# Decode attention with a gated feed-forward: the query projection with x stationary, and two row blocks of the output weight loaded behind the last V piece

## The chip, the cores and the metric

The kernel runs on one core of a Trainium2 chip. Its metric is the device time of one execution in microseconds (us). Most executions of one kernel lie within 0.4 us of its median here, under 0.02%. Differences under 2% count as "the same". A profile's span runs from the first to the last instruction and is about 1.8 us shorter than the device time.

PE is the matrix engine (PEld are its weight loads), DVE the vector engine, ACT the scalar engine, and SP the engine that issues the loads. PSUM is the memory that matmuls write. Each load leaves 16 landing records in the trace, called its shares here; it has landed with the last of them. The granted clock is the part of PE's full clock that the profile shows as granted. The single landing records and DMA packets quoted below are read from the trace itself; no view prints them one by one.

## The reference

One token x (512 values) goes through attention over a cache of 65,536 keys in 32 heads, and through a small gated feed-forward block. A gate g mixes both.

```python
x = A_x                                            # 1 x 1 x 512, bf16
g = sigmoid((x * gate_w).sum(-1))
q = (x @ wq).reshape(32, 128)                      # wq: 512 x 4096
p = softmax(q . k_cache * 128 ** -0.5)             # k_cache, v_cache: 32 x 65536 x 128
a = (p . v_cache).reshape(4096) @ wo               # wo: 4096 x 512
b = (silu(x @ w_gate) * (x @ w_up)) @ w_down       # 512 x 1792, 1792 x 512
out = g * a + (1 - g) * b
```

K and V together are 1,074 MB, the rest is 14 MB. Every byte is used once.

## The kernel before

There are three slots of 64 KB per partition. Each holds one chunk of K or V (32,768 keys, 8 MiB) at a time; every head has two chunks. SP issues all loads but two rows of 1 KB (x and gate_w, issued by ACT) in order, on one queue, and waits for a slot to come free before the next load.

```python
for n in range(N - 1):                 # N = 64 chunks
    load("k", n, [KPP]); load("v", n, [KPP])
    for j in range(0, KPP, m):
        block(n, j, m)                 # DVE: K *= q (in place); PE: identity as weight, 128 products per key summed to 8
        gather()                       # DVE: the sum of these 8; ACT: exp into P_sb
    pv(n)                              # PE: P stationary, 4 keys x 128 columns of V per matmul
```

Before that loop stands the q stage. Slot 0 holds wq, gate and up first; the load of chunk K1 into slot 0 waits until PE has read them. One column of PSUM takes one head; 128 blocks of wq are loaded as weights, with one column of x each:

```python
group("q_ps", [(m_x[:, h : h + 1],
                [(wq_sb[:, t, h * Dh : (h + 1) * Dh], Xc[:, t : t + 1]) for t in range(KT)])
               for h in range(H)], ...)
act("qT", qT, m_x[:, :H], ACT.Copy, ...)
def spread(h):                         # q of one head onto all partitions
    act("dq", dq, ident, ACT.Copy, scale=qT[:, h : h + 1])
    mms("spread", m_sp[:, :Dh], [(ones_b, dq)], ...)
    act("q_bc", q_bc[h % 2], m_sp[:, :Dh], ACT.Copy, ...)
# ... (cut)
gate()     # DVE, PE, ACT: g and 1 - g
hidden()   # PE: 112 matmuls on gate and up
```

At the end, the last V chunk comes in pieces, so that little work stands behind the last landing. The last two V chunks are multiplied by columns: V[:, j, :] is the weight, one column of P is streamed. The heads 0 to 30 go through wo early; only the last head's row block (`wo_last`) waits for the last V:

```python
V_END = [KPP // 2, KPP // 4, KPP // 8, KPP // 16, KPP // 16]      # 128, 64, 32, 16, 16 keys per partition
dma("wd", ...); dma("wo", wo, ...); dma("wl", wo_last[:, 0, :], ...)
load("k", n, [EK] * 4); load("v", n, V_END)
# ... (cut: row_b = (1-g) b; row_a = g * (31 heads) @ wo; rest4 = their sum, turned to 4 x 128)
column(n, V_END[:1]); sum_ps(h, H); norm(h, H)
column(n, V_END[1:], V_END[0])
dve("Z", ...)                                                      # last head's output / its sum
mms("l_ps", m_x[:OT, :P], [(Z[:, OT*q : OT*(q+1)], wo_last[:, 0, P*q : P*(q+1)]) for q in range(OT)], ...)
dve("out_sb", ...)                                                 # g * l_ps + rest4
dma("out", ...)
```

A helper (`Plan`) tracks reads and writes and adds the semaphore waits. It tracks a slot in units of 8 x 128 elements per partition, 2 KB.

The softmax here doesn't subtract the row's maximum and nothing guards it: scores larger than these inputs give would overflow.

## Time and profile before

| | before |
|---|---|
| time | 2518.3 us (2518.23 to 2518.3, 3 runs) |
| span of the profile | 2516.4 us |
| PE / DVE / ACT busy | 79% / 50% / 4% |
| data queue, mean over the span | 432 GB/s, 1088 MB |
| last landing of a load | 2511.84 us |
| start of the last DVE operation | 2513.59 us |

Lines of the page: busy share of the 16 DMA engines in 40 slices (tenths), GB/s in the same slices, and two of the queues (packets, MB, share).

```profile
DMA  9999999999999999999999999999999999999998
GB/s 423 433 433 432 434 435 433 438 433 434 433 433 433 434 435 435 435 433 433 433 433 435 434 433 432 435 436 434 435 433 433 433 433 435 434 436 433 434 433 376
...
q1 hardware_dynamic: 20456, 1087.78, 99.8%
q8 instruction: 12, 0.20, 0.0%
```

Every slice but the last is full. The last one moves 376 instead of about 433 GB/s. The instruction queue carries 12 packets of 16 KB.

The table of windows for stretches of the same run (us; busy time of PE, PEld, DVE, ACT, POOL; granted PE clock; DMA share; GB/s):

```profile
1000.00:2000.00 1000.00, 794.56 (x3430) 157.04 (x1818) 511.97 (x103) 37.76 (x154) 0.00 (x0) 0.91 1.00 434
2508.00:2510.00 2.00, 2.00 (x67) 2.00 (x67) 0.33 (x2) 0.00 (x0) 0.00 (x0) 0.50 0.75 307
2510.00:2512.00 2.00, 1.55 (x59) 1.47 (x56) 0.00 (x0) 0.00 (x0) 0.00 (x0) 0.50 0.17 66
2512.00:2514.00 2.00, 1.22 (x20) 0.76 (x19) 0.57 (x2) 0.00 (x0) 0.00 (x0) 0.50 0.00 0
```

The stream runs at 434 GB/s and thins out over the last 3 us. The landing records show how: the 16 shares of the last transfer land between 2508.82 and 2511.84 us. Had all finished together, that would have been near 2510.1 (the mean of the 16). So by this estimate better balance could give 1.7 us at most. The granted clock in the last 10 us is half.

The timeline of the start (start, duration, engine, what, idle before):

```profile
13.24 3.58 PE L285 MATMUL m_x<-Xc,slot_65 128*128 128x1 bf16 x128 [10.65 <-DMA slot_65<-in_A_wq_dram]
...
23.00 6.85 PE L285 MATMUL m_x<-Xc,slot_65 128*128 128x1 bf16 x112 [5.26 <-DMA slot_65<-in_B_w_up_dram]
29.88 0.33 SPq L181 DMA_DIRECT2D slot_65<-in_A_k_cache_dram  x1
...
32.76 8.69 DVE L344 TENSOR_TENSOR slot_66<-slot_66,q_bc_78 128x16384 bf16<-128x16384 bf16 x1 [1.53 <-DMA slot_66<-in_A_k_cache_dram]
```

PE works on q from 13.24, waits for the up weights until 23.00, and frees slot 0 for K1 at 29.88. The first product starts when the first half of K0 has landed.

The end, from the chain of waits (the chain that ended last, in order of time: start, duration, what):

```profile
2467.34 1.90 issue
...
2470.97 40.88 DMA slot_65<-in_A_v_cache_dram
...
2511.89 0.51 PE m_c L257 x13
...
2512.40 0.25 PE m_c L257 x3
...
2512.68 0.24 DVE Z L601
...
2512.96 0.60 PE m_x L257 x4
...
2513.59 0.34 DVE out_sb L613
```

The 40.9 us of DMA are the time in the queue of the last V piece. Behind its landing stand 16 columns, Z, four matmuls and the last DVE operation. And PE's own lines from the timeline there:

```profile
2507.84 0.18 PE L257 MATMUL m_c<-P_sb_84,slot_65 128*128 128x1 bf16 x1 [2.44 <-issue]
...
2511.89 0.75 PE L257 MATMUL m_c<-P_sb_84,slot_65 128*128 128x1 bf16 x16 [0.45 <-DMA slot_65<-in_A_v_cache_dram]
2512.96 0.59 PE L257 MATMUL m_x<-slot_66,Z 128*4 128x128 bf16 x4 [0.32 <-DVE Z L601]
```

The first line shows 2.44 us for which PE waited for nothing that the profile names. An instruction packet of 16 KB starts at 2505.4 in the DMA records, so PE had probably run out of program. The same happens at 2467.34 in the chain (1.90 us).

### The profile page before, as it was taken

The page shows a single profiled execution, that of the slowest core. Times are in us where ns is not written, and L with a number is a line of the kernel's source. Part 1 is how long each engine was busy: PE and PEld are TensorE (multiplying, and loading weights), DVE is VectorE, ACT ScalarE, POOL GpSimd, SP SyncE. Part 2 cuts the span into 40 slices and gives each one's busy share as a digit, 9 for nine tenths or more (in the row PEclk, how much of TensorE's full clock was granted, in tenths as well). Part 3 has the DMA queues.
Part 4 walks back from the last instruction along what each step waited for, and adds up shares of the span by engine and source line. Part 5 has one row for each costly group of instructions (what it writes and reads, how often), then busy time and mean ns, then how long its engine had stood idle before and what let it go on. Part 6 is the DMA issues. An engine that isn't in the chain of part 4 may idle for free.

```text
span 2516.4 us, 15594 instructions
## 1 busy us (share of the span) xinstructions
PE 1977.2 (79%) x9185; PEld 410.9 (16%) x5221; DVE 1268.3 (50%) x287; ACT 99.1 (4%) x402; POOL 1.9 (0%) x9
## 2 busy tenths in 40 slices
PE   4687877877778778778787787787877877877788
PEld 2111111111111111111111111111111111111113
DVE  3455355464553554645545546445455364464554
ACT  0000000000000000000000000000000000000000
POOL 0000000000000000000000000000000000000000
PEclk9888989989989989898898898998989989989898
DMA  9999999999999999999999999999999999999998
GB/s 423 433 433 432 434 435 433 438 433 434 433 433 433 434 435 435 435 433 433 433 433 435 434 433 432 435 436 434 435 433 433 433 433 435 434 436 433 434 433 376
DMA packets 20478, 1088.02 MB, mean 432 GB/s; under 512 B 2282, under 2 KB 2412, under 8 KB 2668
## 3 DMA queue, kind: packets, MB, share of 16 engines
q1 hardware_dynamic: 20456, 1087.78, 99.8%
q8 instruction: 12, 0.20, 0.0%
q14 instruction: 6, 0.05, 0.0%
q10 hardware_dynamic: 4, 0.00, 0.0%
HBM read 1087.77 MB, written 0.00 MB: 432 GB/s over the span
## 4 chain that ended last, share of the span: by engine, by line
DMA 47%; PE 39%; DVE 13%; ACT 0%; issue 0%; another core or an unknown queue 0%; SPq 0%
PE O_ps L257 17%; DMA slot_67<-in_A_k_cache_dram 16%; DMA slot_66<-in_A_k_cache_dram 15%; DMA slot_65<-in_A_k_cache_dram 14%; PE S_ps_103 L275 11%; PE S_ps_104 L275 9%; DVE slot_67 L344 4%; DVE slot_66 L344 4%; DVE slot_65 L344 3%; DMA slot_65<-in_A_v_cache_dram 2%; PE m_c L257 2%; DVE S_sb_82 L369 2%; PE S_ps_103 L285 1%; ACT P_sb_83 L294 0%; PE S_ps_104 L285 0%
## 5 line engine op out<-in xcount | busy, mean ns | idle before, releaser
L344 DVE TENSOR_TENSOR slot_67<-slot_67,q_bc_79 128x16384 bf16<-128x16384 bf16 (+1 forms) x28 | 208.2, 7469 | 145.4 <-DMA slot_67<-in_A_k_cache_dram 145.4
L369 DVE TENSOR_REDUCE S_sb_82<-S_ps_104 128x128 f32<-128x1024 f32 (+1 forms) x66 | 78.7, 1192 | 395.0 <-PE S_ps_104 L275 395.0
L344 DVE TENSOR_TENSOR slot_65<-slot_65,q_bc_78 128x16384 bf16<-128x16384 bf16 x22 | 190.2, 8688 | 140.5 <-DMA slot_65<-in_A_k_cache_dram 140.5
L344 DVE TENSOR_TENSOR slot_66<-slot_66,q_bc_78 128x16384 bf16<-128x16384 bf16 x22 | 190.3, 8689 | 120.1 <-DMA slot_66<-in_A_k_cache_dram 120.1
L344 DVE TENSOR_TENSOR slot_65<-slot_65,q_bc_79 128x16384 bf16<-128x16384 bf16 x20 | 172.9, 8688 | 120.0 <-DMA slot_65<-in_A_k_cache_dram 120.0
L344 DVE TENSOR_TENSOR slot_66<-slot_66,q_bc_79 128x16384 bf16<-128x16384 bf16 x20 | 172.9, 8688 | 119.2 <-DMA slot_66<-in_A_k_cache_dram 119.2
L344 DVE TENSOR_TENSOR slot_67<-slot_67,q_bc_78 128x16384 bf16<-128x16384 bf16 x20 | 172.9, 8688 | 119.2 <-DMA slot_67<-in_A_k_cache_dram 119.2
L275 PE MATMUL S_ps_103<-slot_67,ident 128*128 128x512 bf16 x680 | 193.8, 455 | 0.0
L275 PE MATMUL S_ps_103<-slot_65,ident 128*128 128x512 bf16 x651 | 186.1, 456 | 0.0
L275 PE MATMUL S_ps_103<-slot_66,ident 128*128 128x512 bf16 x651 | 183.5, 452 | 0.0
L257 PE MATMUL O_ps<-slot_67,P_sb_83 128*4 128x512 bf16 x704 | 153.7, 379 | 21.0 <-ACT P_sb_83 L294 18.3
L257 PE MATMUL O_ps<-slot_66,P_sb_84 128*4 128x512 bf16 x704 | 153.7, 379 | 19.3 <-ACT P_sb_84 L294 19.3
L257 PE MATMUL O_ps<-slot_65,P_sb_84 128*4 128x512 bf16 x640 | 139.7, 379 | 18.3 <-ACT P_sb_84 L294 18.3
L257 PE MATMUL O_ps<-slot_67,P_sb_84 128*4 128x512 bf16 x640 | 139.7, 379 | 18.3 <-ACT P_sb_84 L294 18.3
L257 PE MATMUL O_ps<-slot_65,P_sb_83 128*4 128x512 bf16 x640 | 139.7, 379 | 18.3 <-ACT P_sb_83 L294 18.3
L257 PE MATMUL O_ps<-slot_66,P_sb_83 128*4 128x512 bf16 x640 | 139.8, 379 | 17.5 <-ACT P_sb_83 L294 17.5
L275 PE MATMUL S_ps_104<-slot_67,ident 128*128 128x512 bf16 x680 | 150.7, 379 | 0.0
L275 PE MATMUL S_ps_104<-slot_66,ident 128*128 128x512 bf16 x651 | 143.9, 379 | 0.0
L275 PE MATMUL S_ps_104<-slot_65,ident 128*128 128x512 bf16 x651 | 143.9, 379 | 0.0
L285 PE MATMUL S_ps_103<-slot_65,ident 128*128 128x512 bf16 x21 | 12.8, 608 | 138.0 <-DVE slot_65 L344 138.0
L285 PE MATMUL S_ps_103<-slot_66,ident 128*128 128x512 bf16 x21 | 12.8, 608 | 131.0 <-DVE slot_66 L344 131.0
L285 PE MATMUL S_ps_103<-slot_67,ident 128*128 128x512 bf16 x24 | 13.9, 579 | 125.6 <-DVE slot_67 L344 125.6
(100 smaller groups left out, 720.4 us busy)
## 6 DMA issues: line engine op xcount, KB each, us to landing
slot_66<-in_A_k_cache_dram SPq DMA_DIRECT2D x2, 4096.0 KB, 34.9
slot_67<-in_A_k_cache_dram SPq DMA_DIRECT2D x4, 2048.0 KB, 30.3
slot_65<-in_A_wq_dram SPq DMA_DIRECT2D x1, 4096.0 KB, 12.2
slot_66<-in_A_wo_dram SPq DMA_DIRECT2D x1, 4096.0 KB, 32.4
slot_65<-in_A_v_cache_dram SPq DMA_DIRECT2D x1, 4096.0 KB, 37.1
slot_65<-in_A_v_cache_dram SPq DMA_DIRECT2D x1, 2048.0 KB, 40.3
slot_65<-in_B_w_gate_dram SPq DMA_DIRECT2D x1, 1792.0 KB, 16.0
slot_65<-in_B_w_up_dram SPq DMA_DIRECT2D x1, 1792.0 KB, 21.0
```

What stands on the lines that cost most here:

```text
L257: ins = nc.tensor.matmul(out_ap, lhsT=a, rhs=b, start=start and i == 0, stop=stop and i == len(pairs) - 1,)
L275: ins = nc.tensor.add_instruction(mybir.InstMatmult(name=nc.get_next_instruction_name(), engine=mybir.EngineType.PE, ins=[nc.tensor.lower_ ...
L285: ins = nc.tensor.matmul(out_ap, lhsT=a, rhs=b, start=first, stop=last)
L344: "products", lambda: nc.vector.tensor_tensor(out=w, in0=w, in1=q_rep, op=ALU.mult),
L369: lambda: nc.vector.tensor_reduce(out=S_sb[b][:, :m], in_=S_ps[r][:, :m, :], axis=AXIS.X, op=ALU.add),
```

## The change

Its intent: fewer PE instructions for q, x as the weight and wq streamed; less work and fewer bytes bound to the last V landing, by smaller last pieces and by putting 256 KB of wo behind them, where they may land while PE and DVE finish the last head. To find the space for q4, three one-row tiles share one, and both projections now end in one row. The diff is shortened: `...` and plain words stand for code that is cut.

```diff
-    group("q_ps", ... 32 heads x 4 matmuls, weights wq block, one column of x ...)
-    act("qT", qT, m_x[:, :H], ACT.Copy, ["m_x"], ["qT"])
+    group("q_ps",
+        [[(q_ps[32 * g : 32 * g + 1, i * W : (i + 1) * W],
+           [(x_col, wq_sb[:, t, (2 * g + i) * W : (2 * g + i + 1) * W]) for t, x_col in enumerate(x_cols)])
+          for i in range(2)] ... for g in range(OT)], units(0, 0, WQ) + ["Xc"], [("S_ps", 0)])
+    for g in range(OT):
+        act("q4", q4[32 * g : 32 * g + 1, :], q_ps[32 * g : 32 * g + 1, :], ACT.Copy, ...)
     def spread(h):
-        act("dq", dq, ident, ACT.Copy, ["ident", "qT"], ["dq"], scale=qT[:, h : h + 1])
-        mms("spread", m_sp[:, :Dh], [(ones_b, dq)], ["ones_b", "dq"], ["m_sp"])
+        g, i = divmod(h, QP)
+        act("dq", dq, q4[32 * g : 32 * g + 1, i * Dh : (i + 1) * Dh], ACT.Copy, [("q4", g)], ["dq"])
+        mms("spread", m_sp[:, :Dh], [(ones_b[0:1, :], dq)], ["ones_b", "dq"], ["m_sp"])
...
-    V_END = [KPP // 2, KPP // 4, KPP // 8, KPP // 16, KPP // 16]
+    V_END = [KPP // 2, KPP // 4, KPP // 8, KPP // 16, KPP // 32, KPP // 32]
...
-    dma("wo", wo, ..., units(ws, WO, WL))
+    dma("wo", wo[:, :ON, :], wo_rows[:, :ON, :], units(ws, WO, WO + ON * D))      # ON = H - LATE = 30
     dma("wl", wo_last[:, 0, :], ...)
     load("k", n, [EK] * (KPP // EK))
     load("v", n, V_END)
+    dma("wo2", wo[:, ON:, :], wo_rows[:, ON:, :], units(ws, WO + ON * D, WL))
...
-    row_b and row_a apart, 8 small matmuls for rest4
+    one row: ACT writes (1-g) b, DVE adds g a; 4 small matmuls for rest4
...
     column(n, V_END[1:], V_END[0])
+    mms("late_ps", m_x[:OT, :P], 8 matmuls of ZM with the two late row blocks, stop=False)
     dve("Z", ...)
     mms("l_ps", ..., start=False)
```

More of the change, by code (lines that the diff above doesn't have):

```diff
@@ L18 @@
 VB = 4
+LATE = 2
 R = 8
@@ L122 @@
     slot = [ring_pool.tile([P, SLOT], bf16, name=f"slot{i}") for i in range(SLOTS)]
-    x_row = sb("x_row", [1, D], bf16)
-    gw_row = sb("gw_row", [1, D], bf16)
+    row = sb("row", [1, 3 * D // 2], f32)
+    x_row, gw_row, xg = (row.bitcast(bf16)[:, i * D : (i + 1) * D] for i in range(3))
     ones = sb("ones", [P, P], f32)
@@ L130 @@
     Xc = sb("Xc", [P, KT], bf16)
-    qT = sb("qT", [P, H], f32)
-    dq = sb("dq", [P, Dh], bf16)
+    QP = H // OT
+    q4 = sb("q4", [P, QP * Dh], bf16)
+    dq = sb("dq", [1, Dh], bf16)
     q_bc = [sb(f"q_bc{i}", [P, Dh], bf16) for i in range(2)]
@@ L144 @@
     eg = sb("eg", [P, FT], f32)
-    xg = sb("xg", [1, D], bf16)
     s_t = sb("s_t", [1, 1], f32)
@@ L148 @@
     rest4 = sb("rest4", [OT, P], f32)
-    row_b = sb("row_b", [1, D], f32)
     unit = sb("unit", [1, OT * OT], f32)
     Z = sb("Z", [P, OT * OT], bf16)
+    ZM = sb("ZM", [P, LATE, OT * OT], bf16)
     o_row = sb("o_row", [H, Dh], bf16)
@@ L231 @@
     op("DVE", "unit1", lambda: nc.vector.memset(unit[:, :: OT + 1], 1.0), writes=["unit"])
+    op("DVE", "ZM0", lambda: nc.vector.memset(ZM, 0.0), writes=["ZM"])
     op("DVE", "Z0", lambda: nc.vector.memset(Z, 0.0), writes=["Z"])
@@ L269, in fn @@
             held = None
-            for out_ap, pairs in parts:
-                for i, (a, b) in enumerate(pairs):
-                    first, last = i == 0, i == len(pairs) - 1
-                    if a is held:
-                        ins = nc.tensor.add_instruction(
-                            mybir.InstMatmult(
-                                name=nc.get_next_instruction_name(), engine=mybir.EngineType.PE,
-                                ins=[nc.tensor.lower_ap(b), weights],
-                                outs=[nc.tensor.lower_ap(out_ap)],
-                                start_tensor_calc=first, stop_tensor_calc=last,
-                                tile_size=(P, P), tile_position=(0, 0), ldweights=False,
-                            )
-                        )
-                    else:
-                        ins = nc.tensor.matmul(out_ap, lhsT=a, rhs=b, start=first, stop=last)
-                        weights = ins.ins.ins[1]
-                    held = a
+            for part in parts:
+                part = part if isinstance(part, list) else [part]
+                for i in range(len(part[0][1])):
+                    for out_ap, pairs in part:
+                        a, b = pairs[i]
+                        first, last = i == 0, i == len(pairs) - 1
+                        if a is held:
+                            ins = nc.tensor.add_instruction(
+                                mybir.InstMatmult(
+                                    name=nc.get_next_instruction_name(),
+                                    engine=mybir.EngineType.PE,
+                                    ins=[nc.tensor.lower_ap(b), load.ins[1]],
+                                    outs=[nc.tensor.lower_ap(out_ap)],
+                                    start_tensor_calc=first, stop_tensor_calc=last,
+                                    tile_size=load.tile_size, tile_position=load.tile_position,
+                                    ldweights=False,
+                                )
+                            )
+                        else:
+                            ins = nc.tensor.matmul(out_ap, lhsT=a, rhs=b, start=first, stop=last)
+                            load = ins.ins
+                        held = a
             return ins
@@ L310 @@
     dve("Xc", lambda: nc.vector.tensor_copy(out=Xc, in_=m_x[:, :KT]), ["m_x"], ["Xc"])
+    q_ps = S_ps[0].rearrange("p k r -> p (k r)")
+    W = 512
+    assert QP * Dh == 2 * W
     group(
@@ L315 @@
         [
-            (
-                m_x[:, h : h + 1],
-                [(wq_sb[:, t, h * Dh : (h + 1) * Dh], Xc[:, t : t + 1]) for t in range(KT)],
-            )
-            for h in range(H)
+            [
+                (
+                    q_ps[32 * g : 32 * g + 1, i * W : (i + 1) * W],
+                    [
+                        (x_col, wq_sb[:, t, (2 * g + i) * W : (2 * g + i + 1) * W])
+                        for t, x_col in enumerate(x_cols)
+                    ],
+                )
+                for i in range(2)
+            ]
+            for x_cols in [[Xc[:, t : t + 1] for t in range(KT)]]
+            for g in range(OT)
         ],
-        units(0, 0, WQ) + ["Xc"], ["m_x"],
+        units(0, 0, WQ) + ["Xc"], [("S_ps", 0)],
     )
-    act("qT", qT, m_x[:, :H], ACT.Copy, ["m_x"], ["qT"])
+    for g in range(OT):
+        act("q4", q4[32 * g : 32 * g + 1, :], q_ps[32 * g : 32 * g + 1, :], ACT.Copy,
+            [("S_ps", 0)], [("q4", g)])
     def spread(h):
-        act("dq", dq, ident, ACT.Copy, ["ident", "qT"], ["dq"], scale=qT[:, h : h + 1])
-        mms("spread", m_sp[:, :Dh], [(ones_b, dq)], ["ones_b", "dq"], ["m_sp"])
+        g, i = divmod(h, QP)
+        act("dq", dq, q4[32 * g : 32 * g + 1, i * Dh : (i + 1) * Dh], ACT.Copy,
+            [("q4", g)], ["dq"])
+        mms("spread", m_sp[:, :Dh], [(ones_b[0:1, :], dq)], ["ones_b", "dq"], ["m_sp"])
         q = h % 2
@@ L474, in gate, with project @@
         )
-    def row(key, w_v, names, cols, cname, ks, bank, bname):
+    EARLY = ["x_row", "gw_row", "xg"]
+    def project(key, w_v, names, cols, cname, ks, bank, bname):
         mms(key, bank[0:1, :D], [(cols[:, k : k + 1], w_v[:, k, :]) for k in ks],
@@ L565 @@
     dma("wd", wd, B_w_down.rearrange("(p t) n -> p t n", t=FT), units(ws, 0, WO))
-    dma("wo", wo, A_wo.rearrange("(p t) n -> p t n", t=H), units(ws, WO, WL))
+    wo_rows = A_wo.rearrange("(p t) n -> p t n", t=H)
+    ON = H - LATE
+    dma("wo", wo[:, :ON, :], wo_rows[:, :ON, :], units(ws, WO, WO + ON * D))
     dma("wl", wo_last[:, 0, :], A_wo[(H - 1) * Dh :, :], units(ws, WL, WL + D))
@@ L569 @@
     load("v", n, V_END)
+    dma("wo2", wo[:, ON:, :], wo_rows[:, ON:, :], units(ws, WO + ON * D, WL))
     turn_outputs(0)
     turn_outputs(1)
-    row("b_ps", wd, units(ws, 0, WO), hT, "hT", range(FT), m_x, "m_x")
-    act("row_b", row_b, m_x[0:1, :D], ACT.Copy, ["m_x", "ngval"], ["row_b"], scale=ngval[0:1, :])
-    row("a_ps", wo, units(ws, WO, WL), M, "M", range(H), m_sp, "m_sp")
-    row_a = O_sb[0:1, :D]
-    act("row_a", row_a, m_sp[0:1, :D], ACT.Copy, ["m_sp", "gval"], ["O_sb"], scale=gval[0:1, :])
+    project("b_ps", wd, units(ws, 0, WO), hT, "hT", range(FT), m_x, "m_x")
+    act("row", row[:, :D], m_x[0:1, :D], ACT.Copy, ["m_x", "ngval"], ["row"] + EARLY,
+        scale=ngval[0:1, :])
+    project("a_ps", wo, units(ws, WO, WO + ON * D), M, "M", range(ON), m_sp, "m_sp")
     for i, j in enumerate(range(0, KPP, EK)):
-        if i == 2:
+        if i == 3:
             mms(
@@ L582 @@
                 [
-                    (unit[:, OT * q : OT * (q + 1)], r[:, P * q : P * (q + 1)])
-                    for r in (row_b, row_a)
+                    (unit[:, OT * q : OT * (q + 1)], row[:, P * q : P * (q + 1)])
                     for q in range(OT)
                 ],
-                ["unit", "O_sb", "row_b"], ["m_sp"],
+                ["unit", "row"], ["m_sp"],
             )
@@ L590 @@
         block(n, j, EK)
+        if i == 1:
+            dve(
+                "row2",
+                lambda: nc.vector.scalar_tensor_tensor(
+                    out=row[:, :D], in0=m_sp[0:1, :D], scalar=gval[0:1, :], in1=row[:, :D],
+                    op0=ALU.mult, op1=ALU.add,
+                ),
+                ["m_sp", "gval", "row"], ["row"],
+            )
         while len(todo) > 1:
@@ L593 @@
     gather()
+    for t in range(LATE):
+        dve(
+            "ZM",
+            lambda t=t: nc.vector.tensor_copy(
+                out=ZM[:, t, :: OT + 1], in_=M[:, ON + t : ON + t + 1].to_broadcast([P, OT])
+            ),
+            ["M"], ["ZM"],
+        )
     column(n, V_END[:1])
@@ L597 @@
     column(n, V_END[1:], V_END[0])
+    mms(
+        "late_ps", m_x[:OT, :P],
+        [
+            (ZM[:, t, OT * q : OT * (q + 1)], wo[:, ON + t, P * q : P * (q + 1)])
+            for t in range(LATE)
+            for q in range(OT)
+        ],
+        ["ZM"] + units(ws, WO + ON * D, WL), ["m_x"], stop=False,
+    )
     dve(
@@ L608 @@
         [(Z[:, OT * q : OT * (q + 1)], wo_last[:, 0, P * q : P * (q + 1)]) for q in range(OT)],
-        ["Z"] + units(ws, WL, WL + D), ["m_x"],
+        ["Z"] + units(ws, WL, WL + D), ["m_x"], start=False,
     )
```

## The prediction

> **What bounds the kernel.** The DMA stream. The page's slices show all 16 DMA engines at 9 tenths or more, except in the last slice; its queue part gives 1088 MB at a mean of 432 GB/s over 2516.4 us, and the table of windows shows 433 to 435 GB/s in every stretch from 100 to 2440 us. The Trainium skill ("DMA: Bandwidth & Descriptors", section "Where 436 GB/s comes from") puts the port ceiling of one core at 435 GB/s; the trace agrees. PE is busy 79%, DVE 50%, both with idle time that nobody waits for. The change moves no byte out of the stream, so only the ends can change: before the stream starts (about 2 us, untouched) and after its last landing. In the timeline the last V piece lands at 2511.84 and the span ends at 2516.44, 4.6 us later.
>
> **The start (q).** 128 weight loads with one-column matmuls took 3.58 us (from 13.24). Now 16 loads of x and 32 matmuls of 512 columns. In the trace such matmuls take 0.43 us on a PE coming from idle and 0.22 us later, so I estimate 8 to 10 us, then four one-partition copies on ACT (a 1x512 copy took 0.68 us, so about 1.1 us each). gexp, then the gate/up matmuls, queue behind these copies: they start near 27 instead of 23 us, the second K load is issued near 34 instead of 29.9, the first product starts near 36 instead of 32.8. The queue then still holds over 20 us of transfers (K0 and V0 end near 59). So this stage gets 3 to 4 us slower and costs nothing. The dq copies and spread in the loop are hidden.
>
> **The tail.** Before, after the landing: 16 columns and their wait 0.8 us, Z 0.27, four matmuls to their end 0.6: 1.70 us to the start of the last DVE operation. After: 256 KB of wo land last, at about the same time as the last V piece did, because the bytes are the same. V's last 8 keys land some 0.6 us (256 KB at 434 GB/s) earlier; their columns (8 x 26 ns) and Z fit before or beside the late matmuls. Behind the last landing stand 8 + 4 matmuls of 128 columns, at the 0.106 us start to start that the four had at the 0.50 granted clock there: 1.48 us. Gain about 0.2 us, at most 0.7 with a warm clock; one more DMA and smaller rows cost up to 0.2 us.
>
> **Side effect.** PE's program gets 210 instructions shorter (3088 to 2878). The Trainium skill ("Runtime: NRT & Kernel Launch", section "Instruction fetch mechanics") says blocks of 256 instructions; the trace agrees: PE stands still at the 2304th (2467.3 to 2469.2 us) and the 2816th instruction (2505.4 to 2507.8), with a 16 KB instruction packet each time. Each such packet holds one DMA engine up by about 1.1 us, which spreads the landings of one piece. The stall at 2505 moves to about column 113 of the last 128, where PE waits for V anyway. If that fetch comes late, up to 1.5 us are lost; if its engine is one that already lags, 1 us.
>
> **Time.** 2517.9 us, 2516.3 to 2519.4 eight times in ten. Faster by over 2%: 0.005; within 2%: 0.99; slower: 0.005.
>
> **Right if:** the DMA rate stays 434 GB/s; the first product starts 2 to 5 us later yet K1 and V1 land when they did; the chain of waits ends in the landing of the wo piece, then matmuls, then the output DMA. **Wrong if:** a fetch stall falls behind the last landing, the DMA queue runs dry near 59 or 78 us, or the two-kilobyte rows slow the last slice.

## The result

The changed kernel took 2518.27 us (median of 6 runs, 2517.99 to 2518.45), the kernel before 2518.28 (6 runs, 2518.08 to 2519.59). The ratio is 0.9999 with a 95% interval of 0.9986 to 1.0012: the same. Ratios here are the mean time of one kernel's fast runs over that of the other's of the same rounds, so not quite the ratio of the medians quoted.

The page of the changed kernel, same lines as before:

```profile
DMA  9999999999999999999999999999999999999998
GB/s 423 433 433 432 433 433 434 434 434 434 435 433 433 433 433 438 435 436 433 433 433 433 433 434 433 434 434 433 435 436 433 433 433 433 436 435 435 433 433 376
...
q8 instruction: 11, 0.18, 0.0%
```

The stream has not changed; one instruction packet less. The start in the timeline:

```profile
13.19 0.58 PE L293 MATMUL S_ps<-slot,Xc 128*1 128x512 bf16 x1 [10.62 <-DMA slot<-in_A_wq_dram]
...
14.43 0.63 PE L281 MATMUL S_ps<-slot,Xc 128*1 128x512 bf16 x1
...
14.43 0.58 PE L293 MATMUL S_ps<-slot,Xc 128*1 128x512 bf16 x1
...
18.96 0.38 PE L281 MATMUL S_ps<-slot,Xc 128*1 128x512 bf16 x1
...
19.38 4.13 ACT L302 ACTIVATE q<-S_ps 1x1024 bf16<-1x1024 f32 x4 [16.31 <-PE S_ps L281]
...
23.85 6.86 PE L293 MATMUL m_x<-Xc,slot 128*128 128x1 bf16 x112 [4.20 <-ACT gval L302]
...
30.74 0.33 SPq L183 DMA_DIRECT2D slot<-in_A_k_cache_dram  x1
...
32.86 8.69 DVE L366 TENSOR_TENSOR slot<-slot,q_bc 128x16384 bf16<-128x16384 bf16 x1 [0.77 <-DMA slot<-in_A_k_cache_dram]
```

The 32 matmuls for q run from 13.19 to 19.34; the fourth and the fifth start together at 14.43. The four copies on ACT end at 23.5. The gate and up matmuls start 0.85 us later than before and K1 is issued 0.86 us later. The first product still waits for K0 and starts 0.1 us later. PE's lines at the end:

```profile
2506.52 0.32 PE L260 MATMUL m_c<-P_sb,slot 128*128 128x1 bf16 x6 [0.89 <-DMA slot<-in_A_v_cache_dram]
2507.54 3.70 PE L260 MATMUL m_c<-P_sb,slot 128*128 128x1 bf16 x114 [0.71 <-issue]
...
2512.20 1.01 PE L260 MATMUL m_x<-slot,ZM 128*4 128x128 bf16 x8 [0.32 <-DVE Z L653]
2513.00 0.63 PE L260 MATMUL m_x<-slot,Z 128*4 128x128 bf16 x4
```

PE runs out of program again, but after column 6 of the last 128 instead of at the end of the first 128. The chain of waits at the end:

```profile
2466.35 2.57 issue
...
2471.16 40.30 DMA slot<-in_A_v_cache_dram
...
2511.50 0.39 PE m_c L260 x8
...
2511.91 0.24 DVE Z L653
...
2512.20 1.45 PE m_x L260 x12
...
2513.67 0.34 DVE out_sb L665
```

The chain names the V piece and Z; the last load, two row blocks of wo, landed at 2512.06, and the first late weight load began at 2512.16. Here both came within 0.1 us of each other, and the view names the later semaphore. In the run with the fetch shifted, the late matmuls started at 2512.07, before Z was done (2512.29), so they do not need Z, and it is the wo landing that they wait for. From the last landing to the last DVE operation: 1.75 us before, 1.61 after.

### The profile page after: what moved, and what is told of

The parts are those of the page before. It is cut to its first block, busy times and chain, and to the rows that moved or that the text cites. A ratio compares the mean times of both kernels' runs of the same rounds, so it can differ in the third digit from the quotient of the medians.

```text
span 2516.5 us, 15401 instructions
## 1 busy us (share of the span) xinstructions
PE 1976.6 (79%) x9087; PEld 406.6 (16%) x5107; DVE 1269.1 (50%) x291; ACT 101.9 (4%) x404; POOL 1.9 (0%) x9
## 4 chain that ended last, share of the span: by engine, by line
DMA 47%; PE 39%; DVE 13%; ACT 0%; issue 0%; another core or an unknown queue 0%; SPq 0%
DMA slot<-in_A_k_cache_dram 45%; PE S_ps L281 19%; PE O_ps L260 17%; DVE slot L366 11%; DMA slot<-in_A_v_cache_dram 2%; DVE S_sb L391 2%; PE m_c L260 1%; PE S_ps L293 1%; ACT P_sb L302 0%; PE m_sp L260 0%; SPq L183 0%; PE m_x L260 0%; DVE out_sb L665 0%; DVE Z L653 0%
## 5 line engine op out<-in xcount | busy, mean ns | idle before, releaser
L366 DVE TENSOR_TENSOR slot<-slot,q_bc 128x16384 bf16<-128x16384 bf16 (+1 forms) x132 | 1107.5, 8430 | 768.0 <-DMA slot<-in_A_k_cache_dram 768.0
L281 PE MATMUL S_ps<-slot,ident 128*128 128x512 bf16 x3964 | 999.1, 416 | 0.0
L260 PE MATMUL O_ps<-slot,P_sb 128*4 128x512 bf16 x3968 | 868.1, 379 | 113.1 <-ACT P_sb L302 109.8
L260 PEld LDWEIGHTS O_ps<-slot,P_sb 128*4 128x4 bf16 x3968 | 332.4, 85 | 1054.7 <-issue 357.4
L293 PE MATMUL S_ps<-slot,ident 128*128 128x512 bf16 x132 | 64.7, 490 | 400.1 <-DVE slot L366 400.0
L391 DVE TENSOR_REDUCE S_sb<-S_ps 128x128 f32<-128x1024 f32 (+1 forms) x132 | 157.3, 1192 | 437.5 <-PE S_ps L281 437.0
L293 PEld LDWEIGHTS S_ps<-slot,ident 128*128 128x128 bf16 x132 | 13.2, 100 | 716.9 <-DVE slot L366 706.3
L302 ACT ACTIVATE P_sb<-S_sb 128x128 bf16<-128x128 f32 (+1 forms) x132 | 40.4, 306 | 1421.7 <-DVE S_sb L391 1418.8
L302 ACT ACTIVATE O_sb<-O_ps 4x512 f32<-4x512 f32 x31 | 18.2, 587 | 437.5 <-PE O_ps L260 437.5
L260 PE MATMUL m_c<-pick,O_sb 4*128 4x1 f32 x256 | 32.0, 242 | 0.0
L260 PEld LDWEIGHTS m_c<-pick,O_sb 4*128 4x128 f32 x256 | 31.3, 188 | 3.5 <-issue 3.5
L302 ACT ACTIVATION_READ_ACCUMULATOR P_sb<-S_sb 128x1 f32 x132 | 24.6, 186 | 0.0
L293 PE MATMUL S_ps<-slot,Xc 128*1 128x512 bf16 x16 | 5.7, 567 | 10.6 <-DMA slot<-in_A_wq_dram 10.6
L293 PE MATMUL m_x<-Xc,slot 128*128 128x1 bf16 x112 | 6.9, 198 | 4.2 <-ACT gval L302 4.2
L293 PEld LDWEIGHTS m_x<-Xc,slot 128*128 128x128 bf16 x112 | 6.8, 166 | 4.3 <-issue 4.3
```

Source lines behind the costliest of these rows:

```text
L260: ins = nc.tensor.matmul(out_ap, lhsT=a, rhs=b, start=start and i == 0, stop=stop and i == len(pairs) - 1,)
L281: ins = nc.tensor.add_instruction(mybir.InstMatmult(name=nc.get_next_instruction_name(), engine=mybir.EngineType.PE, ins=[nc.tensor.lower_ ...
L293: ins = nc.tensor.matmul(out_ap, lhsT=a, rhs=b, start=first, stop=last)
L302: "ACT", key, lambda: nc.scalar.activation(out=out_ap, in_=in_ap, func=func, **kw),
L366: "products", lambda: nc.vector.tensor_tensor(out=w, in0=w, in1=q_rep, op=ALU.mult),
L391: lambda: nc.vector.tensor_reduce(out=S_sb[b][:, :m], in_=S_ps[r][:, :m, :], axis=AXIS.X, op=ALU.add),
```

## The experiments

Theory A: the DMA stream sets the time; a start a few us later is swallowed by the queue; the tail gains about 0.2 us. Rival B: the parts move the total by several us each, in opposite directions. The timed runs and the kernel before of the same chip stood together; that kernel's medians were 2518.14 to 2518.21 us.

| run | time, us (median, range) | last landing | landing to last DVE op |
|---|---|---|---|
| before (first profile) | 2518.3 | 2511.84 | 1.75 |
| before again | 2518.16 (2518.14 to 2518.26) | 2511.87 | 1.83 |
| changed | 2518.27 (2517.99 to 2518.45) | 2512.06 | 1.61 |
| changed again | 2518.28 (2517.85 to 2518.33) | 2511.68 | 1.61 |
| old q, new tail | 2518.35 (2518.06 to 2518.44) | 2511.82 | 1.67 |
| new q, old tail | 2518.18 (2517.96 to 2518.34) | 2511.82 | 1.57 |
| old, pieces of 8 keys | 2518.32 (2517.96 to 2518.43) | 2511.89 | 1.56 |
| 12 extra copies | 2518.17 (2517.98 to 2518.23) | 2511.82 | 1.77 |
| 40 extra copies | 2540.62 (one look) | 2534.45 | 1.61 |
| 4 MiB less | 2509.10 (2508.29 to 2510.1) | 2502.12 | 1.61 |
| one late block, shared unit | 2551.37 (2549.76 to 2552.39) | 2511.78 | 33.46 |
| one late block, own unit | 2517.96 (2517.75 to 2518.4) | 2511.72 | 1.52 |
| the same, fetch shifted | 2518.68 (2517.69 to 2519.3) | 2511.94 | 1.18 |
| the same, second time | 2517.80 (2517.58 to 2519.07) | 2511.95 | 1.19 |

### Both kernels once more

No edit.

> The changed kernel once more, to see how far one trace differs from the next. Theory A (the DMA stream sets the time, the change only touches the microsecond behind the last landing): 2518.3 us within 0.3, last landing 2512.06 within 0.3 us, start of the last DVE operation 1.6 us behind it. Rival B (part gains and part losses of some us cancel): the same here, it does not tell them apart.

> The kernel before once more, for the spread of its trace: last landing 2511.84 within 0.2, 1.6 to 1.75 us to the last DVE operation, with a gap of up to 0.2 us at the 14th of the last 16 columns, where the last instruction block begins.

Both held but for two small misses: 1.83 us in the kernel before is 0.08 over the range given, and the changed kernel's last landing at 2511.68 is 0.38 off, not within 0.3. The changed kernel's last landing moved by 0.38 us between its two traces. So a difference of 0.2 us in the last landing, as between the first two traces, is within the spread of one kernel; no cost of one more DMA or of 2 KB rows can be read from it. The time behind the landing repeats much better: 1.61 and 1.61. In the kernel before, the last 16 columns have a gap in both traces, after the 13th: 0.17 and 0.26 us from one matmul's start to the next instead of 0.027. The last instruction block begins there.

### Each part alone

The old q stage in the changed kernel, and the new q stage in the kernel before (there `x_row` and `gw_row` share the space of `row_b`, since q4 did not fit otherwise: 1.1 KB too much per partition).

The diffs in words:

```diff
# old q, new tail: the changed kernel with
-    q_ps = S_ps[0] ...; group("q_ps", 32 matmuls of 512 columns); four copies to q4
+    group("q_ps", 128 one-column matmuls); act("qT", ...)
# new q, old tail: the kernel before with
-    group("q_ps", 128 one-column matmuls); act("qT", ...)
+    q_ps = S_ps[0] ...; group("q_ps", 32 matmuls of 512 columns); four copies to q4
```

> The changed kernel with the old q stage (128 one-column matmuls) and the new tail. Theory A: 2518.3 us within 0.3; the first product starts at 32.8 us as in both kernels, the gate and up matmuls at 23.0 instead of 23.9; the tail as in the changed kernel (1.6 us from the last landing to the last DVE operation). Rival B: the q stage costs or gives over 1 us of the total, so this run leaves 2518.3 by over 1 us. Of the fetch stalls: if blocks count from the program's start, the 209 more instructions move both PE stalls by some 104 columns; if they count from the loop's head, they stay at column 229 of the last but one V chunk and column 6 or 7 of the last 128.

> The kernel before with the new q stage alone (x and gate rows share the space of row_b to make room). Theory A: 2518.3 us within 0.3; tail as before: 1.74 us from the last landing to the last DVE operation, gate and up matmuls at 23.9 us, first product at 32.8. Rival B: off by over 1 us, in the other direction than the run with the old q. Fetch stalls: counted from the loop's head, they stay at column 229 and column 126 or 127 of the first 128; counted from the program's start they move by 104 columns.

Neither part moves the total by over 0.2 us; rival B falls. The first product started at 32.84 and 33.49 us (a small miss in the second run: 32.8 was expected, but gate and up began at 24.69 instead of 23.9 there, and the first half of K0 had landed at 31.72). The PE stall of the last but one V chunk stayed at column 228 or 229 in both, although the programs differ by 209 instructions in front of the loop. So blocks are not counted from the program's start. They fit a count from the loop's head, which the kernel asks to be placed at a fixed slot (`head_slot={PE: 0}`); how it is placed was not measured by itself.

One more expectation missed: with the new q alone, the stall expected at column 126 or 127 was not there, and the instruction packet came at 2496.3 instead of 2505.4 us. By the program's list, the block boundary before it lies in that program two instructions ahead of PE's wait for the last P, so PE would cross it before it waits, and the next block would be under way early. The tail took 1.57 us instead of the 1.74 expected; the gap in the last 16 columns was gone too. The run with the shifted fetch, below, tests this reading.

### Pieces of 8 keys alone

```diff
-    V_END = [KPP // 2, KPP // 4, KPP // 8, KPP // 16, KPP // 16]
+    V_END = [KPP // 2, KPP // 4, KPP // 8, KPP // 16, KPP // 32, KPP // 32]
```

> The kernel before with V's last piece cut in two pieces of 8 keys, nothing else. Theory A: 8 columns of 0.026 us less behind the last landing, 1.53 us instead of 1.74; the landing 0 to 0.2 us later for one more DMA; total 2518.2 within 0.3. If the 0.2 us by which the changed kernel's last landing is later come from cutting the pieces, this run has them too; if from the wo rows behind V, it has not.

1.56 us behind the landing, as expected, against 1.75 before. That gain is no smaller than that of the whole new tail (1.61). With two row blocks of wo last, 8 more matmuls stand behind the last landing in place of the 8 columns and Z of this run; the trade was about even.

### How much the start may slip

```diff
     for g in range(OT): act("q4", ...)
+    for i in range(12):                        # 40 in the second run
+        act("q4", q4[0:1, :], q_ps[0:1, :], ACT.Copy, [("S_ps", 0)], [("q4", 0)])
```

> As the run with 40 extra copies, with 12 (about 12.4 us). Theory A: K1 is issued near 43 us, V1 near 71, both before the queue would run dry (59 and 78 us): 2518.3 us within 0.4 although the first product starts near 45 instead of 32.9. If the start had no slack, 12 us slower.

> The changed kernel with one of the four q copies repeated 40 times, which holds up the gate, and so everything of the start, by about 41 us (a copy takes 1.03 us). Theory A with its slack: the queue holds K0 and V0 until about 59 us and K1 until about 78; K1 would be issued near 72 and V1 near 100, so the queue runs dry for about 13 to 15 us and again for 7 to 9: 20 to 27 us slower. If the start had no slack, it would be 41 us slower; if it never matters, 0.

With 12 extra copies K1 was issued at 42.4, V1 at 70.3, and the first product started at 44.4 instead of 32.9; the time was the same. The queue stayed full, as the table of windows of that run shows:

```profile
60.00:70.00 10.00, 10.00 (x52) 1.08 (x10) 2.87 (x2) 0.85 (x4) 0.00 (x0) 1.00 1.04 452
70.00:80.00 10.00, 8.16 (x39) 3.15 (x38) 1.23 (x1) 0.40 (x2) 0.00 (x0) 1.00 0.97 419
```

With 40, K1 was issued at 72.2 and V1 at 99.4. The same table of this second run shows the queue run dry twice:

```profile
50.00:60.00 10.00, 0.00 (x0) 0.00 (x0) 0.00 (x0) 9.68 (x11) 0.00 (x0) 0.50 0.91 393
60.00:70.00 10.00, 4.70 (x79) 4.73 (x80) 0.47 (x3) 5.03 (x6) 0.00 (x0) 0.50 0.01 2
...
94.00:100.00 6.00, 5.37 (x25) 0.00 (x0) 0.59 (x1) 0.00 (x0) 0.00 (x0) 1.00 0.00 0
```

2 GB/s from 60 to 70 us, nothing from 94 to 100. The cost was 22.4 us for 41 us of delay, inside the 20 to 27 expected, in one look. So the start of this kernel may slip by something over 12 us for nothing; the 0.9 us by which the change delays K1 is far inside. An estimate of the whole slack: V1 was issued 40.8 us later than in the changed kernel (99.4 against 58.6), of which 22.4 were paid, so about 18 us are free.

### 4 MiB less

```diff
+            w = m // 2 if (which, n) == ("v", 30) else m
-                (which, n, at), t[:, at : at + m, :], src[:, at : at + m, :],
+                (which, n, at), t[:, at : at + w, :], src[:, at : at + w, :],
```

> The changed kernel, wrong on purpose: of one of the 64 V chunks only the first half is loaded (4 MiB less; the other half of the slot keeps old values), all work on the engines the same. Theory A: 4.19 MB at 434 GB/s, so 9.7 us less, 2508.6 within 0.6. If PE or DVE work or the latency of the chain from chunk to chunk set the time, much less than that. The output may stay within the tolerance.

The time fell by 9.1 us against the kernel before of the same rounds, with 9.7 expected and runs that spread over 1.8 us. Busy times of the engines were nearly the same (DVE 1269.3 us against 1269.1, PE 1974.1 against 1976.6), as the page of this run shows, and the output stayed within the tolerance:

```profile
PE 1974.1 (79%) x9087; PEld 406.1 (16%) x5107; DVE 1269.3 (51%) x291; ACT 101.9 (4%) x404; POOL 1.9 (0%) x9
```

So the bytes set the time, and the work of PE and DVE did not.

### One late row block

```diff
-LATE = 2
+LATE = 1
```

> The changed kernel with one row block of wo behind V instead of two: 128 KB in rows of 1 KB land last, 4 + 4 matmuls stand behind them instead of 8 + 4. Theory A: from the last landing to the last DVE operation 1.2 us instead of 1.6 (four matmuls of 0.106 us less), the landing within 0.3 us of 2512.06, total 2517.9 within 0.4. If what stands behind the landing did not set the end, there is no change in that interval.

It took 33 us more. The last landing was at 2511.78, as everywhere. What had changed was what waited for it, in PE's lines of the timeline:

```profile
2471.94 5.96 PE L260 MATMUL m_x<-slot,hT 128*1 128x512 bf16 x14
2511.83 8.47 PE L260 MATMUL m_sp<-slot,M 128*1 128x512 bf16 x31 [33.92 <-DMA slot<-in_A_wo_dram]
2520.24 0.39 PE L293 MATMUL S_ps<-slot,ident 128*128 128x512 bf16 x1
```

The early projection (31 matmuls with M) waited for the late load, 33.9 us, and the whole last K chunk stood behind it on PE. Row 30 (early) and row 31 (late) share one 2 KB unit of the helper's tracking, so the projection was made to wait for a load it does not need. With LATE = 2 the cut falls on a unit's edge. The expectation had missed this; the experiment as meant is the next one.

### One late row block in a unit of its own

With `LATE = 1` as before; that the late matmuls read `wo_late` is cut here:

```diff
+    wo_late = view(ws, WL + 2 * D, LATE, D)
+    LU = units(ws, WL + 2 * D, WL + 2 * D + LATE * D)
-    dma("wo2", wo[:, ON:, :], wo_rows[:, ON:, :], units(ws, WO + ON * D, WL))
+    dma("wo2", wo_late, wo_rows[:, ON:, :], LU)
```

> The run with one late row block again, with that block in a tracking unit of its own (the first try put it in the unit that also holds row 30, which the early projection reads; so that projection, and all of the last K chunk behind it on PE, waited for the last landing). Theory A: if that shared unit was the whole cause of the 33 us, the time is back at 2518 or under: last landing 2511.8 within 0.2, then 4 + 4 matmuls, 1.2 to 1.4 us from the landing to the last DVE operation (1.4 if the fetch of the last instruction block, which falls on the first of the last four matmuls here, ends after 2512.4), total 2518.0 within 0.3. If the row form (1 KB rows, 31 KB rows) was the cause, it stays near 2551.

The 33 us were gone: the shared unit was the cause, not the row form. The time behind the landing, 1.52 us, is 0.12 over the range given. PE's lines show where most of the expected gain of 0.4 us over the changed kernel was lost:

```profile
2511.86 0.58 PE L260 MATMUL m_x<-slot,ZM 128*4 128x128 bf16 x4
2512.62 0.58 PE L260 MATMUL m_x<-slot,Z 128*4 128x128 bf16 x4 [0.18 <-issue]
```

Between the fourth late matmul (start 2512.13) and the first of the last four (2512.62) lie 0.49 us instead of 0.11. By the program's list the last instruction block begins exactly there. Its packet started at 2510.3.

### The fetch shifted

On top of the run before:

```diff
-            mms("rest_ps", ...)
+            for _ in range(3): mms("rest_ps", ...)     # same result, 32 more PE instructions
```

> The same with the small rest matmuls issued three times (32 more PE instructions, same result), so that PE crosses a fetch block before it waits for the last P, as it did in the run with the new q alone. Theory A: instruction packets near 2497 and 2508 instead of 2505 and 2510, no stall at column 6 or 7 of the last 128, none among the last matmuls; 1.1 to 1.2 us from the last landing to the last DVE operation; total 2517.8 within 0.3. If fetch blocks don't explain the stalls, nothing changes against the run before.

> The kernel of the run before last once more, because its trace kept to the 1.18 us behind the landing while its five times spread from 2517.7 to 2519.3. Theory A: the trace again has 1.2 us from the last landing to the last DVE operation; the times lie about 2517.8, and the spread was the stream's (the last landing moves from run to run). If the shift itself costs something that the trace of the end doesn't show, the median is again 2518.5 or more.

The trace did what was expected, twice: packets at 2500.4 and 2508.4 or 2508.5 (the first 3 us later than said), no stall at column 6, none at the end. PE's lines of the first of them:

```profile
2506.71 1.81 PE L260 MATMUL m_c<-P_sb,slot 128*128 128x1 bf16 x64 [0.48 <-DMA slot<-in_A_v_cache_dram]
...
2512.07 0.59 PE L260 MATMUL m_x<-slot,ZM 128*4 128x128 bf16 x4
2512.45 0.63 PE L260 MATMUL m_x<-slot,Z 128*4 128x128 bf16 x4
```

From the landing to the last DVE operation it took 1.18 and 1.19 us, against 1.75 before. The block boundaries do set where PE stalls: 32 instructions more moved the packets and removed the stalls of the last chunk. The times, however, fall into two groups: five of the ten runs at 2517.58 to 2517.86 us, below every run of the kernel before, and five at 2518.68 to 2519.3. The ratios to the kernel before are 1.0002 and 1.0001. About 0.6 to 0.9 us of the late group's excess lie outside the program's span: time minus span is 2.28 to 2.57 us there, 1.68 to 1.76 in the early group and mostly 1.7 to 1.8 in the kernel before. What fills it is not shown: both profiled runs belong to the early group. There is a hint only: in the run with the shared unit, one more instruction packet starts at 2549.82, 1.7 us after the end of the span, and there time minus span is 2.5 us. The shifted program has one packet more than the changed kernel too (near 2512 in both traces); but so has the new q with the old tail (at 2516.2), with 1.8 us. No version here beats both kernels clear of the noise.

## Why the prediction was right

The time, 2518.27 us, lies in the range, 0.4 us above the forecast of 2517.9. Point by point:

- **What bounds.** Right, and shown: 4 MiB less took 9.1 us off; 12 us of delay at the start took nothing.
- **The start.** The conclusion was right, the sizes were not. The step that failed is "8 to 10 us" for the 32 matmuls: they took 6.1 (13.19 to 19.34). The estimate put them one after the other. In the trace, matmuls that write different partition groups overlap: the starts fall into four chains of eight, as many as there are groups. They begin at 13.19, 14.43, 15.67 and 16.91, 1.24 us apart, though the first two chains keep 0.43 us from start to start, so that one of them takes over 3 us. (The trace does not print the partitions. But matmuls with a weight load, L293, and without, L281, alternate in the program; they do so within each chain, and not in the list of all starts.) The Trainium skill ("TensorEngine Tiling (Array Packing)", section "Key Properties") says that different tiles can execute in parallel; the trace agrees, and the prediction did not think of it. So gate and up started at 23.85 instead of near 27, and the first product at 32.86 instead of near 36: 0.1 us later than before, not the 2 to 5 that the prediction named as a sign of being right. The other sign held: K1 and V1 landed at 81.0 and 100.4 before, at 81.1 and 100.4 after. The four copies were sized well: 4.13 us against 4.4.
- **The tail.** Predicted from the last landing to the last DVE operation: 1.70 us before, 1.48 after; measured: 1.75 and 1.83 before, 1.61 and 1.61 after. So the gain was 0.14 to 0.22 us, about what was said, though wo behind V did not bring it (pieces of 8 keys alone reached 1.56). It vanishes in the spread of the last landing (2511.68 to 2512.06 for the same kernel). The predicted cost of one more DMA and smaller rows did not show beyond that spread. The step missed is a piece of the old 0.8 us: 0.17 us of it was a fetch gap in the last 16 columns, not columns.
- **The side effect.** "The stall at 2505 moves to about column 113 of the last 128" failed. It moved to column 6. The prediction counted blocks from the program's start, by two stalls of one trace that could not tell this count from another; every trace fits a count from the loop's head, so the instructions saved in front of the loop moved nothing behind it. It cost nothing here, since PE had V to wait for. That was partly luck: the prediction did not see that the next boundary then falls among the late matmuls, behind the last landing.
- **Lagging engines.** The landing records bear out that a packet holds something up by about 1 us. In the changed kernel one of the 16 shares lands 1.2 us behind the others in the pieces up to the packet at 2505.3, and two do from the next piece on. With the fetch shifted, the second joins one piece earlier, behind the packet at 2500.4, and a third behind the one at 2508.4. In the run with the shared unit there is no packet between 2475.6 and 2535, and one share lags to the end. So the added lag follows the packet. It didn't move the last landing (2511.78 in that run), since one share lagged already. The records do not name the engine.
- **The chain.** It was said to end in the wo landing; the view ends in the V piece and Z, 0.08 us later than that landing. The run with the fetch shifted, where Z is still busy when the late matmuls begin, settles which one they need: the wo landing.
- **What could have gone wrong.** The fetch stall behind the last landing was a near miss: it cost 0.1 and 0.2 us in the runs with the old q and with 12 extra copies (the sixth of the late matmuls, where the last block begins), nothing in the two traces of the changed kernel, and a gap of 0.49 instead of 0.11 us in the run with one late block.

## What to carry to other kernels

When the table of windows shows one stream full from start to end, cost a change first by the bytes it moves, then by what stands behind the last landing; everything else can slip by as much as the queue holds, and that slack can be worked out from the issue times (here over 12 us, about 18 by the estimate above). A dependency tracker with coarse units turns a small cut at the wrong place into a wait for the last load: 33 us for one row block, and nothing in the diff shows it. Where PE runs straight-line code of short matmuls, look for "issue" gaps at fixed distances (here 256 instructions or a multiple) and keep the last block boundary away from the critical end.

## What the Trainium skill lacked or had wrong

- "Runtime: NRT & Kernel Launch", section "Instruction fetch mechanics": it gives 16 KiB blocks of 256 instructions, which the traces bear out, and calls the fetch mostly hidden. Here it is not always: each trace has PE stall at column 227 to 229 of one V chunk, 2.1 to 3.1 us from one start to the next, where 128 pairs of weight load and matmul take 3.4 us. It gives no figure for the lead time: in the run with one late block in its own unit, PE went on at 2507.53 past a boundary, the packet for the next block started at 2510.3 and the first matmul of that block ran at 2512.62, about 5 us later. Nor does it say where block boundaries fall after a loop (see the runs with each part alone).
- "DMA: Bandwidth & Descriptors", section "Where 436 GB/s comes from": it says that for transfers from HBM to SBUF the HBM side, about 358 GB/s, binds. With one core at work the traces show 434 GB/s over 1000 us, the 435 that the page gives for the ports. The same paragraph itself names a measured 425 GB/s as near that rate, so the sentence should say for which case the 358 is meant.
- The same page has no figure for how far apart the 16 shares of one transfer end: 3.0 us between the first and the last share of the last transfer in the kernel before, at the end of the kernel, where no later load hides it. Nor does it say that an instruction packet adds to it (see the lagging engines above).
- "TensorEngine Tiling (Array Packing)" gives speedups up to 4x for narrow weights, but no measured time. "TensorE: Matmul & The Clock Gate" has measured speedups of packed matmuls, but none for groups of eight that stand one behind the other in the program, as here: the groups start 1.24 us apart, and all 32 matmuls of 512 columns take 6.1 us, with 0.43 us from start to start within one of the first two groups.
